# Routing operands placed in a PSUM bank, and the expert weight splits assigned to fixed engines, in an attention, dense and expert kernel on one core

## The chip, the cores and the metric

The kernel runs on one core of a Trainium2 chip, as one launch. The metric is the device time of that core in microseconds (us), less is better. The core has TensorE (PE, its weight loads shown as PEld), VectorE (DVE), ScalarE (ACT), GpSimd (POOL) and SyncE (SP, which issues most DMAs). SBUF is the core's main on-chip memory. PSUM is the memory that TensorE writes; the kernel uses eight tiles of 128 x 512 float32 in it, called banks here.

## What is computed

```python
x = attention(q, k, v)                  # 4 x 8 heads, queries pooled by two
x = (x @ w1) * (x @ w2) @ w3 @ w_out    # 2304 tokens, width 512, hidden 1024
logits = x @ w_gate                     # 8 experts
order = np.argsort(-logits.flatten())
...
for idx in order:                       # greedy, 288 tokens per expert
    tok, e = (int(idx) // E, int(idx) % E)
    if assigned[tok] >= 0 or counts[e] >= cap:
        continue
    assigned[tok] = e
    counts[e] += 1
...
for e in range(E):
    mask = assigned == e
    h = np.maximum(x[mask] @ w1[e], 0.0)
    out[mask] = h @ w2[e]
```

## The kernel before, in words

Matrix products of float32 are made of three fast products: each operand is split into a high part (a rounding copy) and a low part (operand minus high part), and high times high, high times low and low times high are accumulated.

Up to about 776 us the kernel computes attention, the hidden layer and the logits. None of that is touched by the change. Then three things run side by side.

**The W and x2 stages** (776 to 953 us). TensorE multiplies w3 by w_out (tiles `Wh`, `Wl`) and then makes the expert input x2 in 18 tiles of 128 tokens. ScalarE makes the high part `x2h`, GpSimd the low part `x2l`; the rows go to DRAM.

**The routing** (`routing`, line 853, 776 to 1168 us). The greedy assignment is done in eight phases, one expert filled per phase. Each of the first seven searches a threshold in eight rounds of four bits (`BITS`, line 770). A round is a chain of small operations: on VectorE `rt_mask` (which tokens reach the 15 candidate thresholds), on TensorE a count, on VectorE `rt_cnt`, `rt_sum`, `rt_own`, on TensorE a sum over partitions, on VectorE `rt_any`, `rt_flag`, `rt_n`, `rt_base`, `rt_thr`, `rt_G` and so to the next `rt_mask`. After the rounds some 25 operations close the phase, among them `rt_ge`, `rt_inc`, `rt_pen` and the update of `rt_U`, and `slot_lists` (line 1069) writes the token list `idx` of the expert. All operands lie in SBUF except the counts that TensorE leaves in PSUM.

**The experts** (`moe_and_experts`, from line 1512; 953 to 1249 us). For each of eight experts the weights come as eight units of 128 x 1024 (`unit`, line 1525): a load into `u` (a ring of three), a high part `uh`, a low part `ul`. The tokens are gathered by GpSimd's indirect DMA (`g`), transposed on TensorE, split into `exh` (ScalarE) and `exl` (VectorE). `expert` (line 1621) accumulates eight tiles of the hidden layer, split into `ehh` (ScalarE) and `ehl` (VectorE, PSUM minus SBUF), then four tiles of the result, evacuated to `ey`, transposed back, evacuated to `eo` and scattered by GpSimd. A unit's `uh` may be on ScalarE or VectorE, its `ul` on VectorE or GpSimd, `ey` and `eo` on ScalarE or VectorE. The units go round 13 places (4 of halves, 9 whole), so weights can be ready about one and a half experts ahead.

**What sets the order.** A planner (`Sched`, line 163) knows a cost for each operation on each engine that may do it, takes on every engine the ready operation of best priority, and writes the result out as a fixed order per engine. Each engine then runs its list in order and waits on semaphores. TensorE's list thus mixes the routing's small matmuls between the expert matmuls at the places where the planner expected their inputs. Routing has a better priority (1900) than experts (3000 and up).

```python
lo_e, hi_e = (("POOL",), ("ACT",)) if first else (("DVE", "POOL"), ("ACT", "DVE"))   # L1537
ps = Hold(s_pt if e == 0 and 4 <= f < AHEAD else sB)                                  # L1626
```

The four banks `pt0` to `pt3` (`s_pt`) serve routing, lists, transposes and, for the first expert, some hidden tiles (`AHEAD`). Four others (`sB`) serve the accumulations.

Of the kernel before, what the change touches and what calls it, by code (L numbers as in the profile page):

```python
# [11 lines left out]
F32 = mybir.dt.float32  # L12
# [14 lines left out]
N = B * SP  # L27
# [825 lines left out]
def routing(nc, sch, rp, slots, c, L, keyL, A, rows_of, idx, prio, prio_l):  # L853
# [6 lines left out]
    def ring(name, n, shape, dt):  # L860
        return make_ring(sch, rp, "rt_" + name, n, shape, dt)

    r_m, r_mu = ring("m", 2, [128, NC], F32), ring("mu", 2, [128, NC], F32)
    r_t8, r_oh = ring("t8", 2, [128, NC, 8], F32), ring("oh", 2, [128, NC, 8], BF16)
    r_mx, r_mask = ring("mx", 1, [128, NC], F32), ring("mask", 2, [128, NC, NTHR], BF16)
    r_flag, r_any, r_n = ring("flag", 2, [128, NTHR], F32), ring("any", 2, [128, NTHR], F32), ring("n", 2, [128, 1], I32)
    r_cnt, r_sum = ring("cnt", 2, [NCG * NTHR, NCG, 8], F16), ring("sum", 2, [NCG * NTHR, 8], F16)
    own8 = rp.tile([97, NTHR, 8], F16, name="rt_own8")
    r_base, r_thr, r_G = ring("base", 2, [128, 1], I32), ring("thr", 2, [128, NTHR], I32), ring("G", 2, [128, NTHR], I32)
    r_M, r_M1 = ring("M", 1, [128, 1], I32), ring("M1", 1, [128, 1], I32)  # L870
    r_ge, r_rows = ring("ge", 1, [128, 2, 8, NC], F32), ring("rows", 1, [128, 16], BF16)
# [6 lines left out]
    r_sc, r_top, r_own = ring("sc", 1, [128, 8], F32), ring("top", 1, [128, 1], F32), ring("own", 2, [128, 8], F32)  # L878
# [22 lines left out]
    lists = slot_lists(nc, sch, rp, slots, c, A, idx, prio, prio_l)  # L901
    for ph in range(8):
# [7 lines left out]
        t8, kt8 = r_t8()  # L910
# [10 lines left out]
        if ph < 7:  # L921
# [89 lines left out]
            inc, kin = r_inc()  # L1011
# [19 lines left out]
            ac, kac = r_acc()  # L1031
# [37 lines left out]
def slot_lists(nc, sch, rp, slots, c, A, idx, prio, prio_l):  # L1069
# [3 lines left out]
    def ring(name, n, shape, dt):  # L1073
        return make_ring(sch, rp, "sl_" + name, n, shape, dt)

    r_all, r_s, r_rows = ring("all", 1, [128, NC, 8], F32), ring("s", 2, [128, NC], F32), ring("rows", 2, [128, 1], BF16)
    r_inc, r_pre, r_slot = ring("inc", 2, [128, NC], F32), ring("pre", 2, [128, 1], F32), ring("slot", 2, [128, NC], F32)
    r_ge, r_g, r_r = ring("ge", 2, [128, NC, 4], F32), ring("g", 2, [128, NC], F32), ring("r", 2, [128, NC], F32)
# [60 lines left out]
def moe_and_experts(tc, sch, env, w1, w2, w3, w_out, w_gate, e1, e2, out):  # L1139
# [277 lines left out]
    routing(nc, sch, rreg, s_pt, rc, L, "L", A, rows_of, idx, P_R, P_L)  # L1417
# [107 lines left out]
    def unit(w, n, k, pr):  # L1525
# [11 lines left out]
        lo_e, hi_e = (("POOL",), ("ACT",)) if first else (("DVE", "POOL"), ("ACT", "DVE"))  # L1537
# [9 lines left out]
        for half in halves:  # L1547
            h, l, _, free = us[i][half or 0]
            n_ = 1024 if half is None else DM
            ss = slice((half or 0) * DM, (half or 0) * DM + n_)  # L1550
            op = split(lambda h=h, n_=n_: h[:, 0:n_], lambda l=l, n_=n_: l[:, 0:n_], lambda raw=raw, ss=ss: raw[:, ss], n_, pr,
                       [("ur", c)], ("uh", i, half or 0), ("ul", i, half or 0), hi_e=hi_e, lo_e=lo_e, free=free if first else ())
            if first:
                pages.first(op)
# [66 lines left out]
    def expert(e, xs, wu, pr):  # L1621
# [26 lines left out]
        for d in range(KD):  # L1648
# [12 lines left out]
            sch.op(None, {"ACT": c_act(CAP), "DVE": c_dve(CAP)}, lambda eng, ps=ps, y=y: evac(eng, y[:, :], ps.tile[:, :CAP]),  # L1661
# [61 lines left out]
AHEAD = 7  # L1723
HELD = 4
LATE = 3
# [5 lines left out]
def attention_moe_experts_kernel(ctx, tc, q, k, v, w1, w2, w3, w_out, w_gate, e1, e2, out):  # L1731
# [10 lines left out]
    for r in regions.values():  # L1742
# [10 lines left out]
           "s_pt": s_pt, "ident": ident, "rc": rc, "xreg": regions["x"], "x2": dpool.tile([N, DM], F32, name="x2"), "x2a": dpool.tile([N, DM // 2], F32, name="x2a"), "w3t": dpool.tile([8, 128, 2, 1024], F32, name="w3t"),  # L1753
# [29 lines left out]
```

## Time and profile before

| | |
|---|---|
| time, median of 3 runs (lowest to highest) | 1267.52 us (1264.34 to 1271.21) |
| the profiled execution's own time | 1259.13 us |
| its span, first to last instruction | 1257.3 us |
| busy: PE, DVE, ACT, POOL | 93%, 83%, 50%, 51% |
| mean granted TensorE clock | 0.977 |

The profiled execution is 1.8 us longer than its span and 8.4 us shorter than the median of the runs. Times inside the trace count from the span's start. Busy shares are averages over stages that have different limits, so the stages are read one by one.

### The profile page before, as it was taken

What the parts mean: (1) busy time and instruction counts of PE and PEld (TensorE: products, weight loads), DVE (VectorE), ACT (ScalarE), POOL (GpSimd) and SP (SyncE); (2) the same over time, 40 slices, a digit from 0 to 9 for tenths busy, and PEclk for the clock granted to TensorE, in tenths of its full rate; (3) what the DMA queues carried; (4) which work ended last, traced back from release to release, by engine and by line L of the source; (5) the groups of instructions that cost most, each with busy time, mean ns of one, the idle gap of its engine ahead of it and who ended that gap; (6) DMA issues with size and microseconds to landing.
All of it is one profiled execution on the core that took longest, in us unless ns stands there. A gap on an engine that the chain in (4) does not pass through costs nothing.

```text
span 1257.3 us, 24260 instructions
## 1 busy us (share of the span) xinstructions
PE 1168.0 (93%) x8377; PEld 1099.2 (87%) x8377; DVE 1042.1 (83%) x2966; ACT 629.3 (50%) x1322; POOL 638.9 (51%) x649
## 2 busy tenths in 40 slices
PE   6999999999999999899999999988898868888997
PEld 4999999999999999899999998766677868888996
DVE  7999999999999999988777876778777988988741
ACT  6888888888888888333222202132221533322321
POOL 4566666666666765444332343264435654453730
PEclk9999999999999999899999999999997989998999
DMA  9676666666666541144555523432224644451620
GB/s 211 148 172 144 156 157 155 153 154 155 155 156 160 119 101 54 62 166 169 185 168 168 185 68 124 154 95 55 57 64 131 219 153 135 143 172 51 226 81 26
DMA packets 116618, 169.88 MB, mean 135 GB/s; under 512 B 47959, under 2 KB 79710, under 8 KB 116494
## 3 DMA queue, kind: packets, MB, share of 16 engines
q1 hardware_dynamic: 113326, 158.89, 46.9%
q0 software_dynamic: 3168, 9.44, 2.3%
q8 instruction: 66, 1.08, 0.4%
q14 instruction: 58, 0.48, 0.1%
HBM read 104.87 MB, written 24.45 MB: 103 GB/s over the span
## 4 chain that ended last, share of the span: by engine, by line
PE 72%; DVE 21%; issue 2%; DMA 2%; POOL 1%; ACT 1%; SPq 0%; DVEq 0%; POOLq 0%; ACTq 0%
PE pb L113 32%; PE s L590 12%; PE pt L614 7%; PE pt L664 6%; PE pt L113 5%; PE s L664 5%; PE s L614 3%; DVE ul L113 2%; DVE cv_v L113 2%; DVE rt_base L113 1%; DVE rt_flag L113 1%; DVE uh L113 1%; DVE rt_own L113 1%; DVE p L600 1%; DVE rt_mask L113 1%
## 5 line engine op out<-in xcount | busy, mean ns | idle before, releaser
L600 DVE TENSOR_SCALAR_CACHE_REDUCE p<-s 128x384 f32<-128x384 f32 x432 | 229.9, 551 | 32.6 <-PE pt L614 12.1
L590 PE MATMUL s<-kst,qst 128*128 128x384 f32 x768 | 198.7, 357 | 7.5 <-DVE p L600 4.0
L605 ACT ACTIVATE p<-p,mn 128x1152 f32<-128x1152 f32 x144 | 181.2, 1258 | 25.3 <-DVE mn L603 23.2
L113 PE MATMUL pb<-xhi,wh 128*128 128x288 f32 x512 | 156.6, 306 | 1.7 <-ACT wh L113 1.7
L113 PE MATMUL pb<-xlo,wh 128*128 128x288 f32 x512 | 152.5, 298 | 2.0 <-DVE xlo L113 2.0
L113 PE MATMUL pb<-xhi,wl 128*128 128x288 f32 x512 | 152.2, 297 | 1.1 <-DVE wl L113 1.1
L590 PEld LDWEIGHTS s<-kst,qst 128*128 128x128 f32 x768 | 122.5, 189 | 14.0 <-DVE p L600 10.6
L614 PE MATMUL pt<-ident,p 128*128 128x128 f32 x879 | 132.1, 272 | 0.3 <-ACT p L605 0.3
L113 POOL TENSOR_TENSOR ul<-u,uh 128x512 fp32r<-128x512 f32 (+1 forms) x45 | 88.9, 1984 | 77.7 <-ACT uh L113 30.2
L648 DVE TENSOR_TENSOR p_lo<-pt,p_hi 128x384 fp32r<-128x384 f32 x230 | 124.6, 551 | 0.7 <-ACT p_hi L331 0.7
L331 ACT ACTIVATE p_hi<-pt 128x384 fp32r<-128x384 f32 x230 | 106.6, 492 | 12.3 <-PE pt L614 12.1
L614 PEld LDWEIGHTS pt<-ident,p 128*128 128x128 f32 x879 | 106.8, 140 | 4.4 <-ACT p L605 0.5
L113 DVE SCALAR_TENSOR_TENSOR cv_v<-cv_raw,cv_v 128x512 int32<-128x512 int32 (+1 forms) x120 | 102.1, 856 | 6.7 <-POOL cv_raw L113 4.6
L113 PEld LDWEIGHTS pb<-xlo,wh 128*128 128x128 f32 x512 | 97.3, 190 | 2.8 <-DVE xlo L113 2.8
L113 PEld LDWEIGHTS pb<-xhi,wh 128*128 128x128 f32 x512 | 97.4, 190 | 2.6 <-ACT wh L113 1.9
L113 PEld LDWEIGHTS pb<-xhi,wl 128*128 128x128 f32 x512 | 97.3, 190 | 1.3 <-DVE wl L113 1.3
L341 POOL TENSOR_TENSOR p_lo<-praw,p_hi 128x384 fp32r<-128x384 f32 x96 | 96.9, 1017 | 0.4
L113 ACT ACTIVATE a<-pb 128x288 f32<-128x288 f32 x64 | 26.2, 410 | 132.4 <-PE pb L113 123.6
L335 POOL CAST p_hi<-praw 128x384 fp32r<-128x384 f32 x96 | 47.5, 506 | 83.3 <-ACT praw L331 83.2
L113 POOL TENSOR_TENSOR cv_raw<-cv_raw 128x512 f32<-128x512 f32 x40 | 43.2, 1079 | 86.5 <-DVE cv_v L113 67.3
L113 PE MATMUL pb<-exh,uh 128*128 128x288 f32 x244 | 78.6, 322 | 6.3 <-DVE ehl L113 6.3
L113 PE MATMUL pb<-ehh,uh 128*128 128x288 f32 x256 | 80.6, 315 | 0.0
(316 smaller groups left out, 3386.3 us busy)
## 6 DMA issues: line engine op xcount, KB each, us to landing
u<-in_moe_w_dram SPq DMA_DIRECT2D x64, 512.0 KB
cv_raw<-in_moe_w_dram SPq DMA_DIRECT2D x32, 512.0 KB
vr<-in_v_dram SPq DMA_DIRECT2D x32, 288.0 KB
kr<-in_k_dram SPq DMA_DIRECT2D x32, 288.0 KB
kst<-kH SPq DMA_DIRECT2D x31, 288.0 KB
kst<-kL SPq DMA_DIRECT2D x31, 288.0 KB
qr<-in_q_dram SPq DMA_DIRECT2D x15, 576.0 KB
w3t<-wg SPq DMA_DIRECT2D x16, 512.0 KB
```

The costliest lines, as they stand in the source:

```text
L113: return f(*[x.get() if isinstance(x, Lazy) else x for x in a], **{n: x.get() if isinstance(x, Lazy) else x for n, x in k.items()})
L331: nc.scalar.activation(out, in_, AF.Copy)
L335: nc.gpsimd.tensor_copy(out, in_)
L341: (nc.vector if eng == "DVE" else nc.gpsimd).tensor_tensor(out, a, b, op=OP.subtract)
L590: nc.tensor.matmul(ps.tile[:, :384], a[:, :], b[:, cs], start=(n == 0), stop=(n == len(passes) - 1))
L600: sch.op("DVE", c_dve(384), lambda ps=ps, c=c, cs=cs: nc.vector.tensor_scalar(t[:, cs], ps.tile[:, :384], 1.0, BIG, op0=OP.mult, op1=OP.mi ...
L605: sch.op("ACT", c_act(S, psum=False, acc=True), lambda: nc.scalar.activation(t, t, AF.Exp, bias=mn[:, 3:4], scale=-1.0, accum_out=sm[0][:, ...
L614: nc.tensor.transpose(ps.tile[:, a * 128:(a + 1) * 128], t[:, b * 128:(b + 1) * 128], ident)
L648: sch.op("DVE", c_dve(384), lambda view=view, src=src: nc.vector.tensor_tensor(view(lo), src(), view(hi).bitcast(F32), op=OP.subtract), us ...
L664: nc.tensor.matmul(ps.tile[:, :n], vt[:, t, :, :], src[half][:, t, off:off + n], start=(half == 0 and t == 0), stop=(half == 1 and t == NT ...
```

## The change

It takes the fourth PSUM bank, `pt3`, out of `s_pt` from the routing on and cuts it into small operands. Most of the routing's and the lists' operands move there, arranged so that an operation with two tensor inputs mostly has one in SBUF and one in the bank; two constants (`grid1`, `wd`) are copied in at the start. Some rings of two become one, the count sums become float32. `s_pt` keeps three banks, and the first expert's early hidden tiles are six in place of seven. For weights of experts 0 to 5 the low part is made on GpSimd alone, for all experts the high part on ScalarE alone, and for experts 0 to 5 `ey` and `eo` on ScalarE alone.

```diff
+def in_bank(bank, name, n, shape, dt, at=None):
+    size = int(np.prod(shape[1:]))
+    if at is None:
+        at = bank[1]
+        bank[1] += n * size
...
+        t = bank[0][:shape[0], at + i * size:at + i * size + size]
...
-    r_m, r_mu = ring("m", 2, [128, NC], F32), ring("mu", 2, [128, NC], F32)
...
+    r_m, r_mu = at("m", 1, [128, NC], F32), at("mu", 1, [128, NC], F32)
+    r_t8p, r_acp, r_incp = (in_bank(bank, "rt_big", 1, [128, NC * 8], F32, 0) for _ in range(3))
...
+    r_flag, r_any, r_n = at("flag", 1, [128, NTHR], F32), at("any", 1, [128, NTHR], F32), ring("n", 2, [128, 1], I32)
+    r_cnt, r_sum = ring("cnt", 2, [NCG * NTHR, NCG, 8], F16), at("sum", 1, [NCG * NTHR, 8], F32)
...
+    r_base, r_thr, r_G = at("base", 2, [128, 1], I32), ring("thr", 2, [128, NTHR], I32), at("G", 2, [128, NTHR], I32)
+    r_M, r_M1 = at("M", 1, [128, 1], I32), ring("M1", 1, [128, 1], I32)
+    (grid1, _), (wd, _) = at("grid1", 1, [128, NTHR], I32)(), at("wd", 1, [128, 8], F32)()
...
+    r_r2, r_pen = ring("r2", 1, [128, 8], F32), at("pen", 1, [128, 8], F32)
+    r_al, r_acc, r_s = at("al", 1, [128, 8], F32), ring("acc", 1, [128, 8, NC], F32), at("s", 1, [128, NC], F32)
...
+    bank = [env["pts"][3], 144]
+    s_pt = Slots(env["pts"][:3])
...
-        lo_e, hi_e = (("POOL",), ("ACT",)) if first else (("DVE", "POOL"), ("ACT", "DVE"))
+        lo_e = ("DVE", "POOL") if n >= BESIDE else ("POOL",)
...
-            sch.op(None, {"ACT": c_act(CAP), "DVE": c_dve(CAP)}, lambda eng, ps=ps, y=y: evac(eng, y[:, :], ps.tile[:, :CAP]),
+            sch.op(None, {"ACT": c_act(CAP)} | ({"DVE": c_dve(CAP)} if e >= BESIDE else {}), lambda eng, ps=ps, y=y: evac(eng, y[:, :], ps.tile[:, :CAP]),
...
-AHEAD = 7
+AHEAD = 6
 HELD = 4
+BESIDE = 6
```

VectorE's list in a round of the routing beside the first expert, before the change. `ul` and `uh` are parts of expert weights, the names with `rt_` belong to the routing:

```order
L113 TENSOR_TENSOR rt_cnt_9240<-pt_66,rc_diag 90x48
L113 TENSOR_REDUCE rt_sum_9246<-rt_cnt_9240 90x8
L113 TENSOR_TENSOR rt_own_9188<-rt_sum_9246,rc_thr 90x120
L113 CAST uh_1_9698<-u_11324 128x512
L113 TENSOR_TENSOR ul_1_9731<-u_11324,uh_1_9698 128x512
L113 TENSOR_REDUCE rt_any_9255<-pt_68 128x15
L113 TENSOR_SCALAR rt_flag_9259<-rt_any_9255 128x15
L113 TENSOR_REDUCE rt_n_9262<-rt_flag_9259 128x1
L113 SCALAR_TENSOR_TENSOR rt_base_9273<-rt_n_9262,rt_base_9316 128x1
L113 SCALAR_TENSOR_TENSOR rt_thr_9275<-rt_n_9262,rt_G_9321 128x15
L113 TENSOR_TENSOR rt_mask_9280<-rt_mu_9208,rt_thr_9275 128x270
L113 CAST uh_1_9720<-u_11360 128x512
```

The same round's kind in the changed kernel; `pt_68` is the bank `pt3`, which now holds the sum, flags, base, G and mu:

```order
L113 TENSOR_TENSOR rt_cnt_9286<-pt_65,rc_diag 90x48
L113 TENSOR_REDUCE pt_68<-rt_cnt_9286 90x8
L113 TENSOR_TENSOR rt_own_9188<-pt_68,rc_thr 90x120
L113 TENSOR_REDUCE pt_68<-pt_66 128x15
L113 TENSOR_SCALAR pt_68<-pt_68 128x15
L113 TENSOR_REDUCE rt_n_9303<-pt_68 128x1
L113 SCALAR_TENSOR_TENSOR pt_68<-rt_n_9303,pt_68 128x1
L113 SCALAR_TENSOR_TENSOR rt_thr_9307<-rt_n_9303,pt_68 128x15
L113 TENSOR_SCALAR pt_68<-rc_g_135,pt_68 128x15
L113 TENSOR_TENSOR rt_mask_9213<-pt_68,rt_thr_9307 128x270
```

The weight parts have left VectorE's list there, and each operation with two tensor inputs now reads one of them from PSUM.

GpSimd's list about the end of the first expert, before (`spacer` and `out_dram` are one scatter, `g` one gather):

```order
L113 DMA out_dram<-eo_11469,idx_9706 2304x512
L113 TENSOR_TENSOR ul_11099<-u_11462,uh_11085 128x1024
L113 TENSOR_TENSOR A<-A,rt_acc_9555 128x144
L113 TENSOR_TENSOR ul_11111<-u_11489,uh_11094 128x1024
L113 TENSOR_TENSOR ul_11204<-u_11541,uh_11181 128x1024
L113 TENSOR_TENSOR ul_11209<-u_11578,uh_11189 128x1024
L113 TENSOR_TENSOR sl_og_9636<-sl_ge_9632 128x54
L113 DMA g_11026<-x_216,idx_11002 96x512
```

And in the changed kernel, where the low parts of every unit in turn stand on it, with the gathers between:

```order
L113 TENSOR_TENSOR ul_11044<-u_11460,uh_11036 128x1024
L113 TENSOR_TENSOR ul_11067<-u_11517,uh_11046 128x1024
L113 TENSOR_TENSOR ul_11104<-u_11616,uh_11052 128x1024
L113 DMA g_10980<-x_216,idx_10490 96x512
L113 DMA g_10999<-x_216,idx_10490 96x512
L113 DMA g_11012<-x_216,idx_10490 96x512
L113 TENSOR_TENSOR ul_11150<-u_11653,uh_11129 128x1024
L113 TENSOR_TENSOR ul_11188<-u_11689,uh_11173 128x1024
L113 TENSOR_TENSOR ul_11225<-u_11720,uh_11207 128x1024
L113 TENSOR_TENSOR ul_11257<-u_11790,uh_11243 128x1024
L113 TENSOR_TENSOR ul_11297<-u_11831,uh_11280 128x1024
```

Before the routing starts the lists of both kernels agree. Over the whole program GpSimd makes 34 whole and 34 half low parts in place of 22 and 23, VectorE 10 and 6 in place of 22 and 17.

## Rows read from the trace of the kernel before

**Rows 1.** The page's 40 equal slices: busy tenths of VectorE, tenths of granted clock.
```profile
DVE  7999999999999999988777876778777988988741
PEclk9999999999999999899999999999997989998999
```
**Rows 2.** Busy time by stage: stretch, length, PE, PEld, DVE, ACT, POOL, clock, DMA.
```profile
776.00:953.00 177.00, 158.84 (x871) 123.04 (x869) 135.60 (x495) 44.26 (x79) 74.44 (x66) 0.98 0.32 89
958.50:1160.00 201.50, 166.11 (x1224) 159.69 (x1224) 176.13 (x478) 64.79 (x122) 99.57 (x83) 0.92 0.44 146
1160.00:1247.00 87.00, 85.43 (x678) 84.50 (x677) 46.95 (x77) 24.95 (x50) 37.10 (x35) 1.00 0.35 114
...
950.00:1000.00 50.00, 40.16 (x286) 37.63 (x285) 41.65 (x115) 15.32 (x31) 31.80 (x24) 0.86 0.58 187
```
**Rows 3.** Waits in 957 to 1160 us: waiter, waited for, total us, times, longest.
```profile
PEld L113 <- DVE rt_mask L113: 18.3, 10, 4.2
...
PE pt L113 <- DVE rt_mask L113: 13.0, 8, 4.0
...
PE pt L113 <- DVE exl L113: 4.1, 2, 2.7
```
**Rows 4.** Timeline of 988 to 994 us: start, duration, engine, operation.
```profile
988.91 2.65 DVE L113 SCALAR_TENSOR_TENSOR rt_base<-rt_n,rt_base 128x1 int32<-128x1 int32 x1
...
989.13 2.41 POOL L113 TENSOR_TENSOR ul<-u,uh 128x1024 fp32r<-128x1024 f32 x1
...
993.10 1.30 POOL L113 TENSOR_TENSOR ul<-u,uh 128x512 fp32r<-128x512 f32 x1 [1.57 <-ACT uh L113]
```
**Rows 5.** Durations by tile in 957 to 1160 us: ns min/median/max, first and last start.
```profile
L113 DVE TENSOR_SCALAR rt_flag<-rt_any x23: 152/174/2083, 958.6 to 1137.6; 128x15 f32<-128x15 f32 x23
...
L113 DVE SCALAR_TENSOR_TENSOR rt_base<-rt_n,rt_base x21: 147/160/2651, 960.6 to 1140.7; 128x1 int32<-128x1 int32 x21
...
L113 DVE SCALAR_TENSOR_TENSOR ehl<-pb,ehh x37: 435/448/458, 975.5 to 1140.3; 128x288 fp32r<-128x288 f32 x37
...
L113 DVE TENSOR_TENSOR rt_cnt<-pt,rc_diag x22: 190/198/205, 963.3 to 1135.3; 90x48 f16<-90x48 f32 x22
```
**Rows 6.** Update of `rt_U`, which closes a phase: start of the first, fourth, seventh.
```profile
813.61 0.17 DVE L113 SCALAR_TENSOR_TENSOR rt_U<-rt_s,rt_U 128x18 f32<-128x18 f32 x1
...
946.19 0.17 DVE L113 SCALAR_TENSOR_TENSOR rt_U<-rt_s,rt_U 128x18 f32<-128x18 f32 x1
...
1148.93 0.17 DVE L113 SCALAR_TENSOR_TENSOR rt_U<-rt_s,rt_U 128x18 f32<-128x18 f32 x1
```
**Rows 7.** VectorE's groups by form, 770 to 937 us: busy us, mean ns, idle before.
```profile
L113 DVE TENSOR_SCALAR rt_flag<-rt_any 128x15 f32<-128x15 f32 x30 | 13.9, 463 | 0.9
L113 DVE TENSOR_TENSOR rt_own<-rt_sum,rc_thr 90x120 f16<-90x120 f16 x30 | 12.8, 428 | 0.9
...
L113 DVE TENSOR_TENSOR rt_pend<-rt_pend,rt_own 128x8 f32<-128x8 f32 x3 | 0.5, 162 | 0.0
...
L113 DVE TENSOR_TENSOR rt_r<-pt,rt_rem 128x8 f32<-128x8 f32 x3 | 0.5, 159 | 0.0
```
**Rows 8.** VectorE's and ScalarE's groups by form, 937 us to the end.
```profile
L113 DVE TENSOR_TENSOR ul<-u,uh 128x1024 fp32r<-128x1024 f32 x22 | 29.9, 1361 | 4.4 <-ACT uh L113 4.2
...
L113 DVE TENSOR_TENSOR ul<-u,uh 128x512 fp32r<-128x512 f32 x17 | 13.3, 785 | 1.8 <-ACT uh L113 0.9 <-DMA u<-in_moe_w_dram 0.8
...
L113 DVE CAST uh<-u 128x1024 fp32r<-128x1024 f32 x14 | 12.5, 891 | 1.8 <-PE pb L113 1.8
...
L113 ACT ACTIVATE uh<-u 128x1024 fp32r<-128x1024 f32 x30 | 31.5, 1057 | 18.5 <-DMA u<-in_moe_w_dram 13.6 <-PE pb L113 4.8
```
**Rows 9.** GpSimd's groups by form, 937 us to the end.
```profile
L113 POOL DMA_INDIRECT out_dram<-eo,idx x24 | 31.4, 1308 | 41.8 <-DVE eo L113 33.9 <-DVE rt_cnt L113 3.4 <-issue 2.8
L113 POOL DMA_INDIRECT g<-x,idx x21 | 22.4, 1068 | 14.4 <-issue 9.3 <-PE pt L113 3.0 <-PE pb L113 0.6
...
L113 POOL TENSOR_TENSOR sl_mv<-sl_og,rc_ids 128x54 bf16<-128x54 f32 x10 | 3.9, 492 | 0.3
```

More of the change, by code (lines that the diff above doesn't have):

```diff
@@ L850, in routing_consts, with nxt, routing @@
     return c
-def routing(nc, sch, rp, slots, c, L, keyL, A, rows_of, idx, prio, prio_l):
+def in_bank(bank, name, n, shape, dt, at=None):
[3 more added lines that the diff above has]
+        bank[1] += n * size
+        assert bank[1] <= 512
+    state = [0]
+    def nxt():
+        i = state[0] % n
+        state[0] += 1
+        t = bank[0][:shape[0], at + i * size:at + i * size + size]
+        t = t if dt == F32 else t.bitcast(dt)
+        t = t if len(shape) == 2 else t.rearrange("p (a b) -> p a b", a=shape[1])
+        return t, (name, i)
+    return nxt
+def routing(nc, sch, rp, slots, bank, c, L, keyL, A, rows_of, idx, prio, prio_l):
     NC = N // 128
@@ L877, in routing @@
     pend, keyP = ring("pend", 1, [128, 8], F32)()
-    r_sc, r_top, r_own = ring("sc", 1, [128, 8], F32), ring("top", 1, [128, 1], F32), ring("own", 2, [128, 8], F32)
+    r_sc, r_top, r_own = at("sc", 1, [128, 8], F32), at("top", 1, [128, 1], F32), at("own", 2, [128, 8], F32)
     def dve(n, fn, r, w, engine="DVE", uses=(), pr=prio):
@@ L899, in pick @@
         return own, ko
-    lists = slot_lists(nc, sch, rp, slots, c, A, idx, prio, prio_l)
+    lists = slot_lists(nc, sch, rp, slots, bank, c, A, idx, prio, prio_l)
     for ph in range(8):
@@ L909, in routing @@
         dve(18, lambda m=m, mu=mu: nc.vector.tensor_tensor(mu, m, U, op=OP.add), [km, keyU], [kmu])
[L910 removed]
+        t8, kt8 = r_t8p()
+        t8 = t8.rearrange("p (c e) -> p c e", e=8)
         dve(144, lambda m=m, t8=t8: nc.vector.tensor_tensor(
@@ L1010, in routing @@
             sch.op("PE", 40, f, r=[kro], takes=ps, prio=prio)
-            inc, kin = r_inc()
+            inc, kin = r_incp()
+            inc = inc.rearrange("p (e c) -> p e c", e=8)
             dve(288, lambda ge=ge, inc=inc: nc.vector.tensor_tensor_scan(
@@ L1067, with slot_lists @@
 RS_PIECES = ((0, 0, 320, 256), (0, 320, 256, 0), (1, 0, 256, 896), (1, 256, 320, 576))
-def slot_lists(nc, sch, rp, slots, c, A, idx, prio, prio_l):
+def slot_lists(nc, sch, rp, slots, bank, c, A, idx, prio, prio_l):
     NC = N // 128
@@ L1074, in ring @@
         return make_ring(sch, rp, "sl_" + name, n, shape, dt)
-    r_all, r_s, r_rows = ring("all", 1, [128, NC, 8], F32), ring("s", 2, [128, NC], F32), ring("rows", 2, [128, 1], BF16)
-    r_inc, r_pre, r_slot = ring("inc", 2, [128, NC], F32), ring("pre", 2, [128, 1], F32), ring("slot", 2, [128, NC], F32)
-    r_ge, r_g, r_r = ring("ge", 2, [128, NC, 4], F32), ring("g", 2, [128, NC], F32), ring("r", 2, [128, NC], F32)
+    at = lambda name, n, shape, dt: in_bank(bank, "sl_" + name, n, shape, dt)
+    r_all, r_s, r_rows = ring("all", 1, [128, NC, 8], F32), at("s", 1, [128, NC], F32), ring("rows", 2, [128, 1], BF16)
+    r_inc, r_pre, r_slot = ring("inc", 2, [128, NC], F32), ring("pre", 2, [128, 1], F32), at("slot", 2, [128, NC], F32)
+    r_ge, r_g, r_r = ring("ge", 2, [128, NC, 4], F32), ring("g", 2, [128, NC], F32), at("r", 1, [128, NC], F32)
     r_oh, r_og = ring("oh", 1, [128, NC, 96], BF16), ring("og", 1, [128, NC, 3], F32)
@@ L1416, in moe_and_experts @@
     rows_of = [rreg.tile([128, 4], I32, name=f"rows{n}") for n in range(8)]
-    routing(nc, sch, rreg, s_pt, rc, L, "L", A, rows_of, idx, P_R, P_L)
+    bank = [env["pts"][3], 144]
+    s_pt = Slots(env["pts"][:3])
+    routing(nc, sch, rreg, s_pt, bank, rc, L, "L", A, rows_of, idx, P_R, P_L)
     sch.label = "W"
@@ L1551, in unit @@
             op = split(lambda h=h, n_=n_: h[:, 0:n_], lambda l=l, n_=n_: l[:, 0:n_], lambda raw=raw, ss=ss: raw[:, ss], n_, pr,
-                       [("ur", c)], ("uh", i, half or 0), ("ul", i, half or 0), hi_e=hi_e, lo_e=lo_e, free=free if first else ())
+                       [("ur", c)], ("uh", i, half or 0), ("ul", i, half or 0), hi_e=("ACT",), lo_e=lo_e, free=free if first else ())
             if first:
@@ L1752, in attention_moe_experts_kernel @@
     env = {"nc": nc, "G": G, "xT": xT, "main": regions["main"], "prep": regions["prep"], "psS": regions["psS"],
-           "s_pt": s_pt, "ident": ident, "rc": rc, "xreg": regions["x"], "x2": dpool.tile([N, DM], F32, name="x2"), "x2a": dpool.tile([N, DM // 2], F32, name="x2a"), "w3t": dpool.tile([8, 128, 2, 1024], F32, name="w3t"),
+           "s_pt": s_pt, "pts": pts, "ident": ident, "rc": rc, "xreg": regions["x"], "x2": dpool.tile([N, DM], F32, name="x2"), "x2a": dpool.tile([N, DM // 2], F32, name="x2a"), "w3t": dpool.tile([8, 128, 2, 1024], F32, name="w3t"),
            "wof": dpool.tile([8, 128, 2, DM], F32, name="wof")}
```

27 lines of the change are left out of this document (13 added, 14 removed).

## The prediction
> **What bounds the kernel now.** I read the page's slices first [rows 1]: VectorE is at nine tenths up to about 570 us, falls, and comes back to eight and nine tenths from 940 to 1160 us, where TensorE's granted clock also has its dips. So I cut the part that the change touches into three stages [rows 2]. In the W and x2 stage (177 us) TensorE is idle for 177 - 158.84 = 18.2 us. [...] Once the routing is over (1160 to 1247 us) it is idle for 1.6 us of 87 at clock 1.00. The last three experts thus take 29 us each, those before 40 us on average (201.5 us for five). The same matmuls ran in both, so the difference is the routing's company.
>
> What does the routing do to TensorE? Its waits [rows 3] name `rt_mask`, the operand of the routing's small matmul, with 18.3 us for weight loads and 13.0 us for matmuls (the two overlap, so they are not added). TensorE's list is fixed: where a small matmul stands and VectorE is late, the expert matmuls behind it stand too. VectorE is busy for 176.13 of 201.5 us there.
>
> Why is it late? At 988.91 us `rt_base`, one element per partition, takes 2.65 us and ends when GpSimd's low part of 2.41 us does [rows 4]. The median of `rt_base` is 160 ns and its longest 2651; of `rt_flag` 174 and 2083 [rows 5]. In the same stretch, beside the same GpSimd work, `ehl` (one input in PSUM, one in SBUF) was never longer than 458 ns and `rt_cnt` (also PSUM and SBUF) never than 205 [rows 5]. So what waits for GpSimd is a VectorE operation with both inputs in SBUF, or a small copy-like one from SBUF to SBUF; what takes one input from PSUM does not wait. It shows in the phases: the first three after 813.61 us took 132.6 us, 44 each, and the next three 202.7 us, 68 each [rows 6].
>
> **The change, part by part.** I work in the time of the profiled execution, 1259.1 us, which is 8.4 us under the median of the runs; the result is moved by that at the end.
>
> (1) *Routing operands in the bank, W and x2 stage.* `rt_flag` took 463 ns in the mean over 30, `rt_own` 428 over 30 [rows 7], against 174 (the median later [rows 5]) and an estimated 273 (`rt_cnt` has 48 elements in 198 ns, `ehl` 288 in 448 [rows 5], so 120 lie at 273). That alone is 30 x 0.29 + 30 x 0.15 = 13 us on the chain; `rt_base`, `rt_G` and others, which now have an operand in the bank, add about as much, so some 25 us over four phases, 44 us to about 38 each. TensorE cannot get back more than its 18.2 us of idle time [rows 2]; I keep 3 of these for waits that any chain of this kind leaves. Gain 15 us (bounds 5 and 18).
>
> (2) *The same, beside the experts, with the weight parts off VectorE.* VectorE loses 12 whole and 11 half low parts (12 x 1.36 + 11 x 0.785 = 25 us), all high parts (14 whole at 0.89, 10 halves taken like a half low part, 20 us) [rows 8], and some 10 us of `ey` and `eo`: 55 us of its 176, apart from its waits for GpSimd. ScalarE takes the high parts at 1.06 us [rows 8], some 21 us, and the evacuations, 9 us; it was busy for 64.8 of 201.5 us [rows 2], so these lie beside other work. With a phase of about 40 us in place of 68 the eighth list is there by about 1070 us, long before the seventh expert needs it, and TensorE's list is no longer held. Recoverable: 35.4 us of idle time and 16 us of clock, 51 us. I leave 5 us for the hand-off (the first gather still ends the x2 stage, and the stretch 950 to 1000 has clock 0.86 [rows 2]), 3 us of idle time at the rate of the last stage (1.6 of 87 us), and 8 us for new waits, on GpSimd above all: 35 us.
>
> (3) *The low parts on GpSimd alone.* From the first gathers to the last low part of expert 5 its list holds 32 whole and 24 half low parts, 18 gathers, 12 scatters and the routing's small work: 32 x 2.41 + 24 x 1.30 [rows 4] + 18 x 1.07 + 12 x 1.31, 9 us of issue (9.3 us for 21 gathers, 2.8 for 24 scatters) and some 5 us for the lists (3.9 for the largest piece of five) [rows 9], together 158 us. TensorE needs that last part after five and a half experts, 5.5 x 29 + 5 = 165 us. So GpSimd must be busy for 96% of the way; it fits with a hair's breadth, and the 8 us in (2) are for this.
>
> (4) *Three banks, six early tiles.* Per expert seven transposes take a bank of `s_pt`. TensorE's wait for `exl` is 4.1 us in two waits [rows 3]; between nothing and that again I take 2 us, inside the 8.
>
> (5) *The rest.* Rings of one instead of two cost nothing where VectorE writes and reads in order; two copies at the start cost 0.3 us at the median of small operations [rows 5]; `rt_inc` and `idx` still have two inputs in SBUF and may wait, some 1 us per phase, hidden behind TensorE's list.
>
> (6) *Reading and writing the bank.* An operation on 8 elements takes 159 ns with a PSUM input and 162 with two SBUF inputs [rows 7]: reading costs nothing. No row has VectorE writing PSUM. I take zero, as the reads are nearest; The bounds are as little below and, above, the 38 ns between `rt_cnt` with a PSUM input and `rt_base` with none [rows 5], charged to PSUM alone: in five steps a round over 56 rounds 11 us of chain, of which perhaps 6 reach TensorE.
>
> [...]
>
> Sum: 1259.1 - 15 - 35 = 1209.1 us for an execution like the profiled one, and with 8.4 us more **1217.5 us** as a median.
>
> **The rivals.**
> *GpSimd becomes the pacemaker (slower).* In its busiest stretch before, 950 to 1000 us, it was busy for 31.8 of 50 us, 64%, in the stage as a whole for 99.6 of 201.5 [rows 2]. If its list, which also waits for ScalarE's high part, for loads in a ring of three and for scatters in order, gets no denser than 64%, 158 us of work take 247, 82 us more than TensorE allows. Then the time is 1217.5 + 82 - 8 (the waits already in the sum) = 1291 us. It decides the sign when the density is below 158 / (165 + 50) = 0.73. For it: the demand of 96%. Against: it was idle before mostly for want of work, with half the low parts elsewhere. Half way, at 0.83, the work takes 190 us, the delay is 25 and the time 1217.5 + 25 - 8 = 1235 us.
>
> *The bank does not free the operations.* If PSUM operands waited as well, GpSimd's doubled low parts would hold the chain more: phases stay at about 60 us beside the experts, (1) gives nothing, and of (2) only what 55 us less on VectorE brings, about a third: 1267.5 - 12 = 1255 us. Against it stand `ehl` and `rt_cnt` [rows 5], never late in 59 tries.
>
> *More than forecast.* If GpSimd keeps up and the clock holds through the hand-off, 8 + 5 us more come back: about 1200 us.
>
> **How the numbers follow.** Forecast as it stands (1205 to 1232): 0.55. More than that (to 1190): 0.13. GpSimd half late (1232 to 1261): 0.17. Bank without effect: 0.05, about half of it within 0.5% of before. GpSimd as the pacemaker: 0.10, of which 0.01 ends near no change. A measurement of this kernel can tell about 0.5%, 6 us, from no change. So faster 0.87, the same 0.04, slower 0.09. The range of 8 in 10 goes from 1195 to 1255 us: it leaves out the slower cases and the best few.
>
> **What would show it.** Right: the longest `rt_flag` and `rt_base` under 0.3 us; `rt_U` every 37 to 42 us throughout; idle time of TensorE in the x2 stage under 6 us; VectorE under 70% beside the experts; GpSimd over 80%; experts 0 to 5 at 28 to 31 us each, the last three as before. Wrong: small operations on the bank still as long as a low part (the bank does not free them), or TensorE waiting for `ul` on GpSimd over 10 us in all (pacemaker), or rounds longer than 4 us with nothing waiting (writing the bank costs).

## The result, and the profile after

The changed kernel took **1225.84 us** (median of 4 runs, 1225.08 to 1233.95) against 1269.37 us for the kernel before in the same session: a ratio of 0.9667, 95% interval 0.9603 to 0.9731. Forecast were 1217.5 us and a range of 1195 to 1255. The profiled execution took 1225.08 us with a span of 1223.3 us; that of before took 1259.1 us. The sum of the prediction said 50 us. Between the medians 43.5 us came (1269.37 - 1225.84), between the two profiled executions 34.0. They differ because the profiled execution of before was a quick one (8.4 us under its median), and that of after lies at its median. The medians are the fairer pair for the whole; only the profiled pair can be split by stage, so the stages below are read from it, and how much of its 16 us of miss is the spread between executions stays open.

The page's slices (busy tenths of VectorE, tenths of granted clock), and busy time by stage with the columns of [rows 2]:

```profile
DVE  7998999999999999997877787676677687785541
PEclk9999999999999999999999999999998989899998
```
```profile
776.00:953.00 177.00, 165.56 (x937) 130.25 (x936) 127.53 (x517) 46.05 (x82) 79.44 (x75) 0.97 0.37 104
...
958.50:1160.00 201.50, 181.68 (x1420) 176.42 (x1419) 143.73 (x434) 98.11 (x182) 145.13 (x122) 0.96 0.53 172
...
1160.00:1213.00 53.00, 53.00 (x410) 52.99 (x409) 18.82 (x34) 14.09 (x29) 8.81 (x14) 1.00 0.17 55
950.00:1000.00 50.00, 44.02 (x338) 41.90 (x338) 37.14 (x135) 24.81 (x45) 36.68 (x29) 0.92 0.45 147
```

In the expert stage TensorE's idle time fell from 35.4 to 19.8 us and its clock rose from 0.92 to 0.96; VectorE went from 87% to 71% busy, GpSimd from 49% to 72%. In the W and x2 stage TensorE is idle for 11.4 us instead of 18.2. Where the 34 us lie is read from GpSimd's first scatter of the first and of the last expert (`out_dram`), before and then after (start, duration, engine, operation):

```profile
1003.05 1.93 POOL L113 DMA_INDIRECT out_dram<-eo,idx  x1
...
1248.87 0.92 POOL L113 DMA_INDIRECT out_dram<-eo,idx  x1 [23.06 <-DVE eo L113]
```
```profile
989.89 0.95 POOL L113 DMA_INDIRECT out_dram<-eo,idx  x1 [0.16 <-issue]
...
1214.90 0.92 POOL L113 DMA_INDIRECT out_dram<-eo,idx  x1 [23.11 <-DVE eo L113]
```

The first expert ends 13.2 us earlier, so much did the stage of W and x2 give. From the first to the last expert it takes 225.0 us instead of 245.8: 20.8 us from the stage of the experts, where I had expected 35. A second trace of the change, from another session, has 231.2 us there, so executions of one kernel differ by some 6 us in this stretch. The distances between the eight experts are 37.4, 38.1, 35.3, 31.1, 29.0, 27.6 and 26.6 us: the first ones are slow, while the routing runs. The updates of `rt_U`, as in [rows 6]:

```profile
812.49 0.18 DVE L113 SCALAR_TENSOR_TENSOR rt_U<-pt,rt_U 128x18 f32<-128x18 f32 x1
...
934.02 0.18 DVE L113 SCALAR_TENSOR_TENSOR rt_U<-pt,rt_U 128x18 f32<-128x18 f32 x1
...
1090.97 0.18 DVE L113 SCALAR_TENSOR_TENSOR rt_U<-pt,rt_U 128x18 f32<-128x18 f32 x1
```

Three phases of 40.5 us, then three of 52.3 (before 44 and 68). What holds the phases beside the experts? VectorE's groups by form (busy us, mean ns, idle before): flag and own from 770 to 937 us as in [rows 7], then from 937 us on. The flag is now `pt<-pt 128x15`, since its tile is the bank; `rt_base` is `pt<-rt_n,pt`.

```profile
L113 DVE TENSOR_TENSOR rt_own<-pt,rc_thr 90x120 f16<-90x120 f32 x32 | 8.8, 275 | 1.0
...
L113 DVE TENSOR_SCALAR pt<-pt 128x15 f32<-128x15 f32 x32 | 5.8, 181 | 1.0
```
```profile
L113 DVE SCALAR_TENSOR_TENSOR idx<-sl_fl 96x3 int32<-96x3 f32 x5 | 13.4, 2679 | 0.1
...
L113 DVE TENSOR_TENSOR_SCAN pt<-rc_rst,rt_ge 128x144 f32<-128x144 f32 x3 | 7.6, 2549 | 0.0
...
L113 DVE TENSOR_SCALAR pt<-pt 128x15 f32<-128x15 f32 x24 | 4.3, 179 | 0.6
...
L113 DVE SCALAR_TENSOR_TENSOR pt<-rt_n,pt 128x1 int32<-128x1 int32 x21 | 3.4, 164 | 0.7
```

No step with an input in the bank waits any more: the flag takes 179 ns, `rt_base` 164. But `idx` (three numbers per partition) takes 2679 ns in the mean, and the scan 2549, although the scan writes its result into the bank. Both have two inputs in SBUF still. In the kernel before these two were at their clean time in the same stretch:

```profile
L113 DVE TENSOR_TENSOR_SCAN rt_inc<-rc_rst,rt_ge 128x144 f32<-128x144 f32 x4 | 1.8, 447 | 0.0
...
L113 DVE SCALAR_TENSOR_TENSOR idx<-sl_fl 96x3 int32<-96x3 f32 x5 | 0.8, 152 | 0.0
```

So some 19 us of waiting (13.4 + 7.6 us, less the 2 us that these steps take clean) turned up in two steps that had waited for nothing in that stretch. The longest `idx` is this one (timeline of VectorE, then of GpSimd):

```profile
1105.76 5.23 DVE L113 SCALAR_TENSOR_TENSOR idx<-sl_fl 96x3 int32<-96x3 f32 x1
1110.92 0.81 DVE L113 SCALAR_TENSOR_TENSOR ehl<-pb,ehh 128x288 fp32r<-128x288 f32 x2
```
```profile
1104.84 1.29 POOL L113 TENSOR_TENSOR ul<-u,uh 128x512 fp32r<-128x512 f32 x1
1106.08 1.29 POOL L113 TENSOR_TENSOR ul<-u,uh 128x512 fp32r<-128x512 f32 x1
1107.32 1.29 POOL L113 TENSOR_TENSOR ul<-u,uh 128x512 fp32r<-128x512 f32 x1
1108.56 2.40 POOL L113 TENSOR_TENSOR ul<-u,uh 128x1024 fp32r<-128x1024 f32 x1
```

`idx` starts during the first low part and ends at 1110.99 us, when the fourth does (1110.96): it let a whole run of GpSimd go by. TensorE's and GpSimd's waits from 940 to 1165 us, with the columns of [rows 3]:

```profile
POOL ul L113 <- ACT uh L113: 31.6, 9, 9.3
...
PE pt L113 <- DVE exl L113: 10.8, 5, 2.8
PEld pt L113 <- DVE exl L113: 9.8, 4, 3.0
...
PEld L113 <- DVE rt_mask L113: 6.6, 6, 3.8
...
PE pt L113 <- DVE rt_mask L113: 4.0, 2, 3.6
```

The wait for `rt_mask` fell from 18.3 to 6.6 us (weight loads) and from 13.0 to 4.0 (matmuls). In its place TensorE waits for `exl`, the low part of gathered rows, which stands behind the routing's steps in VectorE's list (10.8 us, before 4.1). No row has TensorE waiting for a low part of GpSimd; GpSimd itself waits 31.6 us for ScalarE's high parts.

### The profile page after: what moved, and what is told of

Its sections match the earlier page's. It is cut to its first block, busy times and chain, and to the rows that moved or that the text cites. A ratio compares the mean times of both kernels' runs of the same rounds, so it can differ in the third digit from the quotient of the medians.

```text
span 1223.3 us, 24304 instructions
## 1 busy us (share of the span) xinstructions
PE 1161.6 (95%) x8377; PEld 1095.7 (90%) x8377; DVE 971.8 (79%) x2902; ACT 655.9 (54%) x1365; POOL 658.9 (54%) x672
## 4 chain that ended last, share of the span: by engine, by line
PE 78%; DVE 15%; issue 2%; POOL 1%; DMA 1%; ACT 1%; SPq 0%; DVEq 0%; POOLq 0%; ACTq 0%
PE pb L113 37%; PE s L590 12%; PE pt L614 7%; PE pt L113 6%; PE pt L664 6%; PE s L664 5%; DVE pt L113 4%; PE s L614 3%; DVE cv_v L113 2%; DVE sl_oh L113 1%; PE pt L543 1%; DVE p L600 1%; DVE idx L113 1%; DMA z<-y 1%; DMA vr<-in_v_dram 1%
## 5 line engine op out<-in xcount | busy, mean ns | idle before, releaser
L113 POOL TENSOR_TENSOR ul<-u,uh 128x512 fp32r<-128x512 f32 (+1 forms) x68 | 123.9, 1844 | 40.3 <-ACT uh L113 40.0
```

The costliest lines, as they stand in the source:

```text
L113: return f(*[x.get() if isinstance(x, Lazy) else x for x in a], **{n: x.get() if isinstance(x, Lazy) else x for n, x in k.items()})
```

## The experiments

My theory behind the result: what counts is whether a VectorE step on the routing's chain still has the form that waits (two inputs in SBUF, or from SBUF to SBUF); the change freed most of them, and those left over collect the waits. Rivals: the gain comes from VectorE's lighter load, or the steps left are hidden behind TensorE's list. Each ratio is against the kernel before on the same chip. One more rival runs along: an edit can make the planner write another order. The change, the flag alone back in SBUF and `idx` alone have the same order on every engine, so there the step alone differs. In all other pairs the order differs too (with `idx` and scan, some 2390 of TensorE's 2820 matmuls from 770 us on stand in the change's sequence), and that share is not separated.

### The two parts apart

**The bank without the engine part** (three banks and six early tiles as in the change):

```diff
-        lo_e = ("DVE", "POOL") if n >= BESIDE else ("POOL",)
+        lo_e, hi_e = (("POOL",), ("ACT",)) if first else (("DVE", "POOL"), ("ACT", "DVE"))
...
-            sch.op(None, {"ACT": c_act(CAP)} | ({"DVE": c_dve(CAP)} if e >= BESIDE else {}), lambda eng, ps=ps, y=y: evac(eng, y[:, :], ps.tile[:, :CAP]),
+            sch.op(None, {"ACT": c_act(CAP), "DVE": c_dve(CAP)}, lambda eng, ps=ps, y=y: evac(eng, y[:, :], ps.tile[:, :CAP]),
...
```

> The change without its engine part: routing operands in the bank, three banks in s_pt, six early tiles, but high and low parts of weights, ey and eo placed by the planner as before. Theory (the waits for GpSimd are what costs, and the bank ends them): rt_flag and rt_base never above 0.3 us, the x2 stage keeps its whole gain (the x2 stage ends at about 940 us), and about half of the gain beside the experts stays, since VectorE keeps 55 us of weight parts that themselves wait for GpSimd: about 1240 us, ratio 0.977. Rival (taking work off VectorE is what pays, the bank alone does little beside the experts): only the x2 stage's 13 us stay, about 1255 us, ratio 0.99.

Measured: 1231.08 us, ratio 0.9715 (0.9666 to 0.9764), 9 us better than the theory, and the rival's 1255 us falls. Its expert stage, the two steps from 937 us on, and TensorE's wait from 957 to 1160 us:

```profile
958.50:1160.00 201.50, 178.99 (x1383) 171.81 (x1383) 167.52 (x491) 74.56 (x140) 110.38 (x96) 0.95 0.50 167
```
```profile
L113 DVE TENSOR_TENSOR_SCAN pt<-rc_rst,rt_ge 128x144 f32<-128x144 f32 x3 | 3.7, 1236 | 0.0
...
L113 DVE SCALAR_TENSOR_TENSOR idx<-sl_fl 96x3 int32<-96x3 f32 x5 | 1.8, 365 | 0.1
```
```profile
PEld L113 <- DVE rt_mask L113: 2.7, 6, 1.0
```

The first three phases are those of the full change (40.6, 40.6, 40.3 us); from the first to the last expert it takes 230.7 us. The phases beside the experts take 70.1, 57.8 and 58.8 us, longer than in the full change, and yet TensorE waits for `rt_mask` for 2.7 us only. So the length of a phase does not tell by itself what TensorE waits.

**The engine part without the bank** (the diff the other way round, on the kernel before, four banks):

> The kernel before with the engine part alone: low parts for experts 0 to 5 on GpSimd, high parts on ScalarE, ey and eo of experts 0 to 5 on ScalarE; all routing operands in SBUF, four banks. Theory: GpSimd is denser, so rt_flag, rt_base, rt_G and their like wait more often beside the experts, phases stay over 50 us, and the gain of the lighter VectorE is mostly given back: 1252 to 1275 us, ratio 0.985 to 1.005. Rival (VectorE's load is what counts): most of the gain beside the experts is there, 1238 us or less, ratio 0.975 or less.

Measured: 1295.82 us, ratio **1.0237** (1.0199 to 1.0275), slower, and worse than the theory's own band. Its expert stage, two of VectorE's groups from 937 us on (before, then here), and TensorE's wait from 957 to 1200 us:

```profile
958.50:1160.00 201.50, 141.91 (x990) 134.54 (x991) 160.03 (x412) 64.33 (x118) 114.10 (x90) 0.84 0.34 118
```
```profile
L113 DVE TENSOR_SCALAR rt_flag<-rt_any 128x15 f32<-128x15 f32 x26 | 13.3, 513 | 0.4
...
L113 DVE TENSOR_TENSOR rt_own<-rt_sum,rc_thr 90x120 f16<-90x120 f16 x26 | 9.2, 354 | 0.5
```
```profile
L113 DVE TENSOR_SCALAR rt_flag<-rt_any 128x15 f32<-128x15 f32 x27 | 31.9, 1183 | 0.7
L113 DVE TENSOR_TENSOR rt_own<-rt_sum,rc_thr 90x120 f16<-90x120 f16 x27 | 20.9, 772 | 0.7
```
```profile
PEld L113 <- DVE rt_mask L113: 35.2, 12, 7.0
```

VectorE did lose its weight parts, yet the flag rose from 513 ns to 1183, `rt_own` from 354 to 772, and TensorE's wait for `rt_mask` doubled. These two steps took 30.3 us more, the kernel 28.1 (1295.82 - 1267.76). Here a lighter VectorE was worth nothing while its small steps stood behind a denser GpSimd. The two parts do not add: alone they give 0.9715 and 1.0237, together 0.9667.

**Three banks and six early tiles alone:**

```diff
+    s_pt = Slots(env["pts"][:3])
...
-AHEAD = 7
+AHEAD = 6
...
```

> The kernel before with three banks in s_pt from the routing on and six early tiles, nothing else: the price of the bank. Theory: between no difference and 3 us more, ratio 0.997 to 1.005. Rival (transposes and routing matmuls queue for banks): 8 us more or worse, ratio 1.007 and up.

Measured: 1264.32 us, ratio 0.9977 (0.9956 to 0.9998). The bank taken from the transposes costs nothing; TensorE's wait for `exl` from 940 to 1165 us is 3.9 us there, with four banks 4.1.

**The flag alone back in SBUF,** the rest of the change kept:

```diff
-    r_flag, r_any, r_n = at("flag", 1, [128, NTHR], F32), at("any", 1, [128, NTHR], F32), ring("n", 2, [128, 1], I32)
+    r_flag, r_any, r_n = ring("flag", 2, [128, NTHR], F32), ring("any", 2, [128, NTHR], F32), ring("n", 2, [128, 1], I32)
```

> The changed kernel with two operands of one step, any and flag, back in SBUF, so that rt_flag is again an operation from SBUF to SBUF. Theory: rt_flag alone waits again, mean 0.4 us or more in place of 0.18 over 56 of them with single ones near 2.4 us, all others stay short; 10 to 15 us more on the routing chain, of which TensorE sees about half: 1232 us, some 0.5% slower than the changed kernel, ratio to before about 0.971. Rival (the operations are short because VectorE is lighter, not because of the bank): rt_flag stays at 0.18 us and the time at 1226 us.

Measured: 1249.04 us, ratio 0.9871 (0.9826 to 0.9916), about 23 us more than the change, where I had expected 6. Its flag, from 937 us on:

```profile
L113 DVE TENSOR_SCALAR rt_flag<-rt_any 128x15 f32<-128x15 f32 x24 | 26.8, 1115 | 0.6
```

That is 24 x (1115 - 179) ns = 22.5 us beside the experts, and 7 us more in the x2 stage (402 ns in place of 181, over 32). The scan, in turn, is clean again beside the experts (456 ns, 6.3 us less). Together 23 us, and the time shows about that: 23 us between the medians, 18 to 26 us by the ratios, as the change is taken from its second or its first session. One step of 15 elements carries about half of the change's gain; what waited on this chain was here paid about in full.

### The steps that were left

**`idx` reads its high digit from PSUM,** where it comes from, and not from its copy:

```diff
-        dve(3, lambda: nc.vector.scalar_tensor_tensor(idx[n], fl[:, 0], 256.0, fl[:, 1], op0=OP.mult, op1=OP.add),
-            [kf], [("idx", n)])
+        dve(3, lambda: nc.vector.scalar_tensor_tensor(idx[n], ps2.tile[:96, 0:3], 256.0, fl[:, 1], op0=OP.mult, op1=OP.add),
+            [kf], [("idx", n)], uses=[ps2])
```

> The kernel after, with one input of idx (the step that turns the list's PSUM sums into row numbers) read straight from PSUM instead of from its SBUF copy; the values are the same. After, five of these one-element steps took 13.4 us beside the experts (longest 5.2 us). Theory (what still has all its inputs in SBUF is what still waits for GpSimd, and it is the reason why phases beside the experts take 52 us and not 40): idx falls to under 0.3 us each and the phases beside the experts to about 50 us, the time to about 1220 us (1216 to 1224, 2 to 10 us under after). Rival (hidden: TensorE is held by something else): idx falls as well, the time stays at 1225 +- 3 us.

**The scan too:** the equality mask goes into the bank, the scan's result into SBUF, and the reduction of both masks becomes two.

```diff
...
-    r_t8p, r_acp, r_incp = (in_bank(bank, "rt_big", 1, [128, NC * 8], F32, 0) for _ in range(3))
+    r_t8p, r_acp, r_gep = (in_bank(bank, "rt_big", 1, [128, NC * 8], F32, 0) for _ in range(3))
...
-                ge[:, 1].rearrange("p e c -> p (e c)"), 0.0, op0=OP.mult, op1=OP.add), [(kge, 1)], [kin])
+                gp.rearrange("p e c -> p (e c)"), 0.0, op0=OP.mult, op1=OP.add), [kgp], [kin])
...
```

> As idx_only, and one input of the routing's scan (the equality mask) is put in the bank too, at the price of a reduction that is split in two (about 0.25 us more per phase). After, three scans took 7.6 us beside the experts instead of 1.4. Theory: scan and idx both at their clean time (under 0.6 and under 0.3 us), phases beside the experts at 46 to 49 us, the time about 1217 us (1212 to 1222). Rival (hidden): phases get shorter by the same few us but the time stays at 1225 +- 3 us, because TensorE's fixed list or the clock sets it.

**The same without the engine part** (the diff of the first experiment on top):

> As idx_scan, with the engine part of the change taken back: weight parts and results of all experts go where the planner puts them, six early transpose tiles still. It tells what the engine part is worth once nothing on the routing's chain waits for GpSimd. The bank without the engine part was 5 us slower than after (1231 against 1226 us). Theory (the engine part helps by taking work off VectorE, its price being long GpSimd operations that hold idx and the scan): with that price gone the engine part is worth more than before, so this kernel is 5 to 12 us slower than idx_scan. Rival (the engine part only moves work): within 3 us of idx_scan.

**The change once more,** beside these three:

> The kernel after once more, beside the other three on one chip, so that differences of a few us can be read: 1225 us (1222 to 1229), 0.966 to 0.970 of before.

Measured, on one chip (before: 1264.65 us):

| kernel | us | ratio | interval | phases beside the experts, us |
|---|---|---|---|---|
| the change | 1230.17 | 0.9727 | 0.9693 to 0.9762 | 52.5, 55.2, 52.0 |
| with `idx` | 1217.99 | 0.9631 | 0.9597 to 0.9665 | 52.7, 47.8, 48.6 |
| with `idx` and scan | 1211.47 | 0.9582 | 0.9548 to 0.9617 | 48.5, 44.7, 43.9 |
| these, without the engine part | 1226.38 | 0.9692 | 0.9658 to 0.9726 | 59.9, 61.1, 60.0 |

The change itself stands 4 us higher than in its first session (the two intervals overlap), so the table's rows are compared with each other. `idx` alone is worth 12.2 us where 2 to 10 were expected, with the scan 18.7 where 8 were, and the rival "hidden" falls. `idx` alone leaves the order as it was, so its 12.2 us are the step's. The scan's 6.5 us hold a new order too: the phases of the x2 stage also fall, from 40.5 to 39.0 us, where the scan had waited little (589 ns in the mean). The two steps from 937 us on and the expert stage with both freed, then the stage without the engine part:

```profile
L113 DVE TENSOR_TENSOR_SCAN rt_inc<-rc_rst,pt 128x144 f32<-128x144 f32 x3 | 1.3, 440 | 0.0
...
L113 DVE SCALAR_TENSOR_TENSOR idx<-pt,sl_fl 96x3 int32<-96x3 f32 x5 | 0.8, 150 | 0.1
```
```profile
958.50:1160.00 201.50, 192.50 (x1517) 186.97 (x1516) 129.45 (x436) 106.59 (x198) 148.83 (x128) 0.97 0.54 180
```
```profile
958.50:1160.00 201.50, 181.06 (x1411) 174.16 (x1410) 171.02 (x492) 75.51 (x138) 104.27 (x95) 0.97 0.50 168
```

21.0 us of VectorE's time in two steps became 2.1, TensorE's idle time in the stage 9.0 us instead of 19.8, and from the first to the last expert it takes 210.4 us (990.42 to 1200.8) instead of 225.0 in the first trace of the change and 231.2 in the second, taken beside these; with `idx` alone it takes 218.4. So the two steps, with the new order, hold 14.6 to 20.8 us, at least what step (2) had missed by (35 - 20.8 = 14.2).

The engine part is worth 14.9 us here (1226.38 to 1211.47), a little more than the 5 to 12 expected. On the bank alone it was worth nothing that can be measured (0.9715 without it, 0.9667 and 0.9727 with it in two sessions), and on the kernel before it cost 2.4%. The same edit had three results; they follow how many steps of the chain still waited for GpSimd, though each time the planner's order changed as well.

### The halves of the engine part, and how far it goes

All four stand on the kernel with `idx` and scan freed. **Only the low parts** of the first six experts on GpSimd alone, high parts and results (these as in the first experiment) where the planner puts them:

```diff
-                       [("ur", c)], ("uh", i, half or 0), ("ul", i, half or 0), hi_e=("ACT",), lo_e=lo_e, free=free if first else ())
+                       [("ur", c)], ("uh", i, half or 0), ("ul", i, half or 0), hi_e=("ACT",) if first else ("ACT", "DVE"), lo_e=lo_e, free=free if first else ())
...
```

> idx_scan with one half of the engine part alone: low parts of the first six experts on GpSimd only, high parts and results where the planner puts them. The whole engine part took idx_scan from 1226 to 1211 us. Theory (what counts is VectorE's time; of the 55 us that the engine part takes from it, the low parts are 25): about 7 of the 15 us are left, 1219 us (1215 to 1223). Rival (a low part of 1.4 us is the longest step that a routing round stands behind, so these alone matter): 1211 to 1214 us.

**Only high parts and results** on ScalarE:

```diff
-        lo_e = ("DVE", "POOL") if n >= BESIDE else ("POOL",)
+        lo_e = ("POOL",) if first else ("DVE", "POOL")
```

> idx_scan with the other half of the engine part alone: high parts and results of the first six experts on ScalarE only, low parts shared by VectorE and GpSimd as before. Theory (VectorE's time counts; high parts and results are 30 of the 55 us): about 8 of the 15 us are left, 1218 us (1214 to 1222). Rival (the low parts alone matter): 1224 to 1228 us.

The whole part for **all eight experts**:

```diff
-BESIDE = 6
+BESIDE = 8
```

> idx_scan with the engine part for all eight experts in place of six. Theory (the engine part pays while the routing needs VectorE; it is over by about 1090 us, and 16 more whole low parts of 2.4 us fall on GpSimd, which at 29 us an expert it cannot all do): the last two experts are 3 to 8 us slower each, 1218 to 1226 us in all. Rival (GpSimd keeps up, as it did for six): 1211 +- 3 us.

And the kernel that they stand on, once more:

> idx_scan once more beside these, so that differences of a few us can be read: 1211 us (1208 to 1215), 0.955 to 0.962 of before.

Measured (before: 1268.73 us): low parts only 1217.19 us, 0.9590 (0.9556 to 0.9625); high parts and results only 1216.36 us, 0.9581 (0.9547 to 0.9614); both 1210.31 us, 0.9536 (0.9504 to 0.9569); all eight experts **1206.34 us, 0.9504** (0.9471 to 0.9536). With one half missing the kernel is 6.9 or 6.1 us slower than with both, so the rival, that the low parts alone matter, falls. The theory fits: VectorE is busy for 171.0 of 201.5 us without the engine part, for 146.7 with the low parts moved, 154.8 with the others and 129.5 with both. The new orders are not separated from that, and the phases beside the experts do not go with the time (49.3, 46.5, 45.5 us with the low parts, 61.1, 56.2, 48.5 with the others). The expectation for all eight experts was wrong. GpSimd's share of the stage rose to 86% and no engine's waits name it:

```profile
958.50:1160.00 201.50, 195.48 (x1547) 190.40 (x1546) 113.16 (x422) 107.38 (x196) 174.14 (x142) 0.97 0.53 180
```

The low parts that I counted as too many were 15 (10 whole, 5 half), all that VectorE still had, and the distance between the fifth and the sixth expert fell from 29.1 to 25.0 us. The 4 us between six and eight experts lie inside the overlap of the intervals against before; the runs themselves do not overlap (1203.18 to 1206.78 against 1208.12 to 1212.00). This version is faster than both kernels of the case.

## Why the prediction was right, and where it was not

The verdict was right (faster, inside the range), and so was its reason: the steps that waited for GpSimd were among those without an input in PSUM, and an input in the bank freed them (the flag's mean went from 463 ns in the x2 stage and 513 beside the experts to 181 and 179). Of the signs that were to show it, the longest flag and `rt_base` came (182 and 165 ns) and the last three experts. Phases beside the experts, TensorE's idle time, the shares of VectorE and GpSimd (71% and 72%) and the experts while the routing runs all fell short. By its own steps:

**(1) x2 stage: 13 us for a forecast of 15.** The flag went from 463 to 181 ns and `rt_own` from 428 to 275 (the estimate was 273), which is the 13 us of chain that I counted. A phase took 40.5 us, not 38, and TensorE kept 9.1 us idle of 776 to 940 us (164 - 154.90), the most of it in waits for `rt_oh` and the list's `sl_rows`; before, it was 17.1 us. So 8.0 of the 13 us are idle time; the granted clock, 0.98 there before and 1.00 after, gave as an estimate 3 us of the rest (164 x 0.02), which the step had left out. "I keep 3 of these for waits that any chain of this kind leaves" was too little.

**(2) Beside the experts: 21 us for a forecast of 35.** This is the step that failed, and (5) is where. The prediction let the phases shrink to 40 us and put the waits of `rt_inc` and `idx` at "some 1 us per phase, hidden behind TensorE's list". They were some 19 us, and not hidden: freeing `idx` alone, in the same order, gave 12.2 us. Before, both had run clean beside the experts (152 and 447 ns), while other steps of the round did the waiting; with those freed and GpSimd denser, the steps that were left ran into its low parts. In the terms of the sum, 15.6 of the 35.4 us of idle time (201.5 - 166.11 [rows 2]) came back. No run shows the 16 us of clock as time lost; it can stand as an estimate, 201.5 x (1 - 0.92) [rows 2], and what the runs showed is a mean granted clock that went half of the way, from 0.92 to 0.96. The second half of the error: 35 us stood behind "VectorE loses 55 us", and the engine part gave none of it as the change stands; bank alone and full change differ by less than can be measured.

**(3) GpSimd's list: no bound.** Forecast was 96% of the way busy, with 8 us of waits. GpSimd was 72% busy; no engine's waits name it, and what stood behind its low parts were `idx` and the scan. The work was sized about right (160.7 us busy from the first gather, 943.3 us, to its last low part, 1175.3). But the 165 us assumed experts of 29 us; TensorE took 35 to 38 for the first ones, so the demand of 158 us in 165 was never made, and the change itself stayed at a density of 0.72, under the rival's 0.73. The version for all eight experts comes nearest: 86%, and still no wait. So "GpSimd becomes the pacemaker" did not happen here up to 86%; at 96% it is untried.

**(4) Three banks, six early tiles: nothing** for a forecast of 2 us (ratio 0.9977). The new wait for `exl`, 10.8 us, is not the bank's: with three banks and nothing else it is 3.9 us. With `idx` alone freed 9.4 us of it are left, with `idx` and the scan 4.0.

**(6) Reading and writing the bank: 4 to 5 ns a step, for a forecast of zero.** `rt_base` on the bank takes 164 ns in the mean, against a median of 160 in [rows 5]; the flag 179 against 174.

**The rivals.** "The bank does not free the operations" is refuted by the flag in both directions (179 ns in the bank, 1115 back in SBUF, in the same order). "More than forecast" did not come; `idx`, scan and the engine part for all experts reach 1206 us, by three edits that the change did not have.

What is still open: with both steps freed the third and fourth expert take 33.5 and 34.5 us, the last 26.6, and phases beside the experts 44 to 48 us against 39. VectorE is then 64% busy and no step of it stands out; I read it as plain occupancy, which was not tried further.

## What to carry to other kernels

When one engine's small steps wait for another, list every step of the chain that can wait, not those that do: here, once the worst were freed, the waits moved to the rest (the scan and `idx`, 2.6 us beside the experts before, 21.0 us after), and a row that showed a clean time before was no price for after. Here, moving work to the engine that is waited for paid only once these steps were freed: the same move cost 2.4%, then gave nothing, then gained 1.2%. An input in a spare PSUM bank was the way to get there, and giving up the bank cost nothing (ratio 0.9977).

## What the runs showed of the hardware

A VectorE step with two SBUF inputs waited for more than one GpSimd instruction here. In the changed kernel the scan, two inputs in SBUF, took up to 2948 ns, the flag, from bank to bank, never over 182, and `idx`, two inputs in SBUF, stayed for 5.23 us behind the rest of one low part and three more, issued back to back (each starts 0.05 us before the one in front of it ends). With a denser list on GpSimd a single wait got longer still: the longest flag took 2083 ns before [rows 5], and 7.53 us with the engine part alone.

GpSimd's instructions stretched as well. Its whole low parts took 2581 ns in the mean before, 2619 with the bank alone, and with the change (first row):

```profile
L113 POOL TENSOR_TENSOR ul<-u,uh 128x1024 fp32r<-128x1024 f32 x34 | 80.9, 2399 | 33.4 <-ACT uh L113 33.1
...
L113 POOL DMA_INDIRECT out_dram<-eo,idx x24 | 23.1, 964 | 43.8 <-DVE eo L113 36.1 <-ACT eo L113 4.0 <-issue 3.5
```

The mean hides how: the median is 2407 ns before and 2397 after. Before, 7 of the 22 took 2.67 to 3.43 us, and each of these began while VectorE was in a weight part of its own, as here (VectorE's low part, then GpSimd's, both before):

```profile
978.94 1.22 DVE L113 TENSOR_TENSOR ul<-u,uh 128x1024 fp32r<-128x1024 f32 x1
```
```profile
978.95 3.43 POOL L113 TENSOR_TENSOR ul<-u,uh 128x1024 fp32r<-128x1024 f32 x1 [1.92 <-DVE rt_base L113]
```

After, where VectorE makes no high parts there and its low parts only from 1123 us on, none took over 2.50 us. A scatter's issue got shorter too: 964 ns in the mean instead of 1308 [rows 9], by a longest of 1.44 us instead of 4.74, at medians of 926 and 934.
